# Retention, routed experts and a SoLU layer on one core: router products and masked score products on quarters of the array, two kinds of copies in ScalarE's queue

## The chip, the core and the metric

The kernel runs on one core of a Trainium2 chip. A core has TensorE (matmuls, which read SBUF and write PSUM), VectorE, ScalarE and GpSimd (element-wise work), SyncE (which here issues DMAs), and DMA engines that move data between HBM and SBUF. Each engine takes its own instructions in order; they wait for one another by semaphores. The metric is the time of one execution on the device, in microseconds (us).

## The reference, cut to what matters

Three layers follow one another: retention (attention with a decaying mask and no softmax), a layer of eight experts with one expert per token, and a dense layer with a SoLU and a normalisation. All is 32-bit floating point.

```python
# q, k, v: batch 8, heads 8, sequence 576, head_dim 64
scores = scale * np.matmul(q, k.transpose(0, 1, 3, 2))
Dmat = np.where(rel >= 0, gamma[:, None, None] ** rel[None, :, :], 0.0)
ret = scores * Dmat[None, :, :, :]
attn = np.matmul(ret, v)                      # -> x: 4608 tokens x 512

logits = x @ w_gate                           # 8 experts
expert_idx = np.argmax(logits, axis=1)
gate_w = softmax(logits)[np.arange(N), expert_idx]
out[mask] = gate_w[mask, None] * (np.maximum(x[mask] @ w1[e], 0.0) @ w2[e])   # per expert e

h = x @ w_in                                  # third layer, x is now `out`
e = np.exp(h - h_max); sm = e / (np.sum(e) + 1e-09); solu = h * sm
return ((solu - mu) / np.sqrt(var + 1e-06) * g_ln) @ w_out
```

## The kernel before, in words

**Chunks.** The retention runs over 8 batches of 576 tokens. A batch is cut into four chunks of 128 tokens and a fifth of 64, so there are 40 chunks, n = 0 to 39. The decay lets the mask be split: what a chunk's queries see of earlier chunks goes through a running state (64 x 64 per head), and only the square of a chunk with itself is computed as scores. For each chunk TensorE makes, in this order of the program:

- `scores(n + 1)`, one chunk ahead (line 448): keys by queries for eight heads into two PSUM tiles `ps`; VectorE multiplies each by its part of the decay table, PSUM to SBUF, giving `pp` (line 451, for the 64-token chunk line 453). The two `ps` tiles are all there are, so the next scores wait for that;
- state products (line 481): the state `old` by the scaled queries `qp`, into `po`; not in the first chunk of a batch;
- masked score products (line 493): the values by `pp`, added into the same `po`. Per head these contract over the 128 keys of the chunk and give 64 rows by 128 queries. The decay table is zero where a key comes after the query;
- the state update `upd` (line 472): keys by values into `pu`, which stays in PSUM over a batch; VectorE copies it to SBUF as the next state (line 474). The fifth chunk has none;
- `px` for one token tile (line 528), in `xtile`.

`po` has one buffer. ScalarE copies it to the token tiles `xts` (line 504): a tile holds 128 tokens with features in partitions. In even batches a chunk is just one tile; in odd batches it is the second half of one tile and the first half of the next, in two copies.

**`xtile`** turns a finished tile and finds its expert logits in one go: `xts` is the stationary operand, and the moving operand `wgi` holds, for each block of 128 features, an identity (128 columns) beside the gate weights (8 columns). `px` is tokens by 136 columns per block. A matmul contracts over 128 features and gives 64 tokens, so two of them fill the two column halves of the array. ScalarE copies `px` to `xr` (line 529) in two pieces, each with its own PSUM buffer. A tile is `ready` for this when all its tokens come before the current chunk. `xtile` is called at the end of `chunk(n)`.

**`route`** handles tiles in groups of 8, 8, 8, 4, 4 and 4: it sums the partial logits (line 539), picks the expert, ranks the tokens and builds index lists. It is a generator: `tick(budget)` runs some of its steps on VectorE at the end of each chunk and again after it, each step priced by hand (0.15, or 0.35 for one scaled tile), and a step that needs TensorE waits for the next chunk ("pe"). In `scale` (lines 562 to 584) each tile is multiplied by its gate into `xo`, by ScalarE (line 576) for even tiles and by VectorE (line 578) for odd ones, except in the last group, where ScalarE does all; SyncE then issues the store of a whole group to HBM (line 583). SyncE's queue also holds the chunk loads, `load(n + 7)` after each chunk.

GpSimd scales the keys (line 424) and queries (line 430) of chunk n + 2 in `prep`. From the index lists GpSimd gathers the tokens of each expert (line 368), and the experts (lines 867 to 884) and the third layer follow on TensorE. Some lines: 203, 592 to 596 and 241 are route's small matmuls, 682 and 701 to 702 build `wgi`, 178 and 179 split an expert's weights in two parts.

## Time and profile before

| what | value |
|---|---|
| median of 3 runs | 1051.08 us (1048.8 to 1055.26) |
| the profiled execution's own time | 1045.0 us |
| its span | 1043.2 us |
| TensorE matmuls busy | 1012.7 us, 97% of the span |
| VectorE busy | 648.1 us, 62% |
| ScalarE busy | 449.5 us, 43% |
| GpSimd busy | 231.1 us, 22% |
| mean granted TensorE clock | 0.992 |
| data moved by DMA | 130.79 MB |

The span is from the first to the last instruction of one profiled execution; its own time has some 2 us around that. In the profile PE is TensorE's matmuls, PEld its weight loads (each matmul has one, loaded while an earlier matmul runs), DVE is VectorE, ACT ScalarE, POOL GpSimd, SP SyncE; a q behind the name is the engine's sequencer. L448 is line 448. A matmul of 32-bit data appears as two loads and two matmuls. The retention takes about the first 170 us.

### The profile page before, as it was taken

The page shows a single profiled execution, that of the slowest core. Times are in us where ns is not written, and L with a number is a line of the kernel's source. Part 1 is how long each engine was busy: PE and PEld are TensorE (multiplying, and loading weights), DVE is VectorE, ACT ScalarE, POOL GpSimd, SP SyncE. Part 2 cuts the span into 40 slices and gives each one's busy share as a digit, 9 for nine tenths or more (in the row PEclk, how much of TensorE's full clock was granted, in tenths as well). Part 3 has the DMA queues.
Part 4 walks back from the last instruction along what each step waited for, and adds up shares of the span by engine and source line. Part 5 has one row for each costly group of instructions (what it writes and reads, how often), then busy time and mean ns, then how long its engine had stood idle before and what let it go on. Part 6 is the DMA issues. An engine that isn't in the chain of part 4 may idle for free.

```text
span 1043.2 us, 20687 instructions
## 1 busy us (share of the span) xinstructions
PE 1012.7 (97%) x8110; PEld 918.3 (88%) x8110; DVE 648.1 (62%) x1642; ACT 449.5 (43%) x847; POOL 231.1 (22%) x254
## 2 busy tenths in 40 slices
PE   7999998899999999999999999899999999999997
PEld 6888887899999999999999997788888888888885
DVE  3467777634677787988343427766666666566652
ACT  1344344333344443433333326455545555545542
POOL 3636421210010102010100021332322222322211
PEclk9999999999999999999999999899999999999999
DMA  9977873344363535453423231111112111111001
GB/s 338 367 263 292 328 267 113 109 156 141 116 206 113 177 122 192 140 187 133 140 102 115 93 109 41 47 51 41 51 41 61 49 43 41 51 42 41 31 21 43
DMA packets 51814, 130.79 MB, mean 125 GB/s; under 512 B 6504, under 2 KB 21344, under 8 KB 47872
## 3 DMA queue, kind: packets, MB, share of 16 engines
q1 hardware_dynamic: 45664, 109.98, 30.1%
q0 software_dynamic: 6048, 19.44, 5.6%
q8 instruction: 66, 1.08, 0.4%
q14 instruction: 36, 0.29, 0.1%
HBM read 99.95 MB, written 29.44 MB: 124 GB/s over the span
## 4 chain that ended last, share of the span: by engine, by line
PE 75%; DVE 3%; issue 2%; ACT 1%; DMA 1%; POOLq 0%; POOL 0%; ACTq 0%
PE py L882 21%; PE ph L867 19%; PE pf L1170 16%; PE hx L1072 7%; PE hz L1072 4%; PE hy L1072 4%; PE ptl L1155 3%; PE px L850 2%; DVE wof L1112 1%; DMA x<-xd,src 0%; ACT raw L1115 0%; DVE wof L1085 0%; DMA out_dram<-o__11948,dst 0%; DMA out_dram<-o__12050,dst 0%; ACT raw L1104 0%
## 5 line engine op out<-in xcount | busy, mean ns | idle before, releaser
L882 PE MATMUL py<-hh,wh 128*128 128x344 f32 (+7 forms) x512 | 157.6, 308 | 0.0
L882 PE MATMUL py<-hl,wh 128*128 128x344 f32 (+7 forms) x512 | 154.7, 302 | 0.0
L882 PE MATMUL py<-hh,wl 128*128 128x344 f32 (+7 forms) x512 | 154.5, 302 | 0.0
L368 POOL DMA_INDIRECT x<-xd,src x42 | 43.5, 1036 | 330.6 <-PE px L850 270.9
L869 ACT ACTIVATE hh<-ph 128x344 fp32r<-128x344 f32 (+7 forms) x128 | 54.1, 425 | 116.4 <-PE ph L867 113.6
L179 DVE TENSOR_TENSOR wl<-raw,wh 128x1024 fp32r<-128x1024 f32 x64 | 78.2, 1221 | 31.2 <-ACT wh L178 30.4
L882 PEld LDWEIGHTS py<-hh,wh 128*128 128x128 f32 x512 | 96.4, 188 | 0.1
L882 PEld LDWEIGHTS py<-hh,wl 128*128 128x128 f32 x512 | 96.5, 188 | 0.0
L882 PEld LDWEIGHTS py<-hl,wh 128*128 128x128 f32 x512 | 96.2, 188 | 0.0
L867 PE MATMUL ph<-xh,wh 128*128 128x344 f32 (+7 forms) x512 | 93.7, 305 | 1.3 <-ACT xh L853 1.3
L867 PE MATMUL ph<-xl,wh 128*128 128x344 f32 (+7 forms) x512 | 93.5, 305 | 0.0
L867 PE MATMUL ph<-xh,wl 128*128 128x344 f32 (+7 forms) x512 | 93.4, 305 | 0.0
L870 DVE SCALAR_TENSOR_TENSOR hl<-ph,hh 128x344 fp32r<-128x344 f32 (+7 forms) x128 | 60.1, 471 | 51.0 <-ACT hh L869 50.9
L884 ACT COPY yo<-py 128x344 f32<-128x344 f32 (+7 forms) x64 | 26.4, 413 | 134.8 <-PE py L882 104.8
L1170 PE MATMUL pf<-woh,wh 128*128 128x512 f32 x288 | 76.9, 409 | 4.6 <-ACT wh L1157 4.6
L1170 PE MATMUL pf<-wol,wh 128*128 128x512 f32 x288 | 81.3, 405 | 0.0
L867 PEld LDWEIGHTS ph<-xh,wh 128*128 128x128 f32 x512 | 78.4, 189 | 1.6 <-ACT xh L853 1.5
L1158 DVE TENSOR_TENSOR wl<-ptl,wh 128x512 fp32r<-128x512 f32 x72 | 49.5, 688 | 47.7 <-ACT wh L1157 47.6
L867 PEld LDWEIGHTS ph<-xl,wh 128*128 128x128 f32 x512 | 78.5, 189 | 0.5 <-DVE xl L854 0.5
L867 PEld LDWEIGHTS ph<-xh,wl 128*128 128x128 f32 x512 | 78.4, 189 | 0.0
L1170 PE MATMUL pf<-woh,wl 128*128 128x512 f32 x288 | 71.9, 391 | 0.0
L178 ACT CAST wh<-raw 128x1024 fp32r<-128x1024 f32 x64 | 67.0, 1047 | 0.0
(604 smaller groups left out, 2080.8 us busy)
## 6 DMA issues: line engine op xcount, KB each, us to landing
raw<-in_w_dram SPq DMA_DIRECT2D x64, 512.0 KB
kc<-in_kvc_dram SPq DMA_DIRECT2D x30, 1024.0 KB
yg<-yd SPq DMA_DIRECT2D x72, 128.0 KB
xd<-xo SPq DMA_DIRECT2D x3, 2048.0 KB
f<-in_win_dram SPq DMA_DIRECT2D x16, 256.0 KB
f<-in_wout_dram SPq DMA_DIRECT2D x16, 256.0 KB
kc<-in_kq_dram SPq DMA_DIRECT2D x8, 256.0 KB
xd<-xo SPq DMA_DIRECT2D x2, 1024.0 KB
```

Source lines behind the costliest of these rows:

```text
L178: nc.scalar.copy(wh, raw)
L179: V.tensor_tensor(out=wl, in0=raw, in1=wh.bitcast(F32), op=ALU.subtract)
L368: nc.gpsimd.indirect_dma_start(out=x[:w, i, :], out_offset=None, in_=xd[:rows, :], in_offset=bass.IndirectOffsetOnAxis(ap=src[:w, e * CT + ...
L867: nc.tensor.matmul(ph, w[:, w0 + kb * P:w0 + kb * P + P], xx[:, kb, cc], start=(n == 0), stop=(n == 3 * KD - 1))
L869: nc.scalar.activation(out=hh[:, cc], in_=ph, func=AF.Relu)
L870: V.scalar_tensor_tensor(out=hl[:, cc], in0=ph, scalar=0.0, in1=hh[:, cc].bitcast(F32), op0=ALU.max, op1=ALU.subtract)
L882: nc.tensor.matmul(p, w[:, ff], h[:, cc], start=(n == 0), stop=(n == 3 * NFB - 1))
L884: nc.scalar.copy(yo[:, cc], p)
L1072: nc.tensor.matmul(p, x[:, 2 * a + k], m[:, w, k], start=(first and k == 0 and i == 0), stop=(k == 1 and i == 2), skip_group_check=True)
L1155: nc.tensor.transpose(p[:, kb, :], u[:, f * P:f * P + P], ident)
L1158: V.tensor_tensor(out=ll[:, fs, :], in0=p, in1=lh[:, fs, :].bitcast(F32), op=ALU.subtract)
L1170: nc.tensor.matmul(pfs[t], a[:, f, :], w[f // 2][:, f % 2, :], start=(n == 0), stop=(n == m - 1))
```

## The change

The quarters: a matmul that contracts over 64 rows and gives 64 rows of output uses a quarter of the array, and four of them can stand in it side by side.

- `px`: each block of 128 features is taken as two halves of 64 features; the identity in `wgi` is 64 wide, so a block has 72 columns instead of 136. Sixteen matmuls on quarters take the place of eight on halves. The logits are now the sum of eight parts instead of four, and the features of a tile stand in another order, which the layout of the experts' first weights (made on the host) follows. `px` is one PSUM tile of two banks instead of two of one.
- masked score products: the first 64 queries of a chunk see only its first 64 keys, so their products contract over 64 keys, on quarters (`av_soon`); the last 64 queries keep all 128 keys (`av_late`). The host swaps the two halves of the keys of odd heads, so that the first keys lie in the other partitions.
- `upd` copies the state with ScalarE instead of VectorE.
- `scale` multiplies all tiles with ScalarE.
- `xtile` is called ahead of `chunk(n)`, behind `scores(n + 1)`, instead of at its end.
- `wgi` needs no zeros, and two copies instead of four.

```diff
-        ps_x = ax.enter_context(tc.tile_pool(name="ps_x", bufs=2, space=PSUM))
+        ps_x = ax.enter_context(tc.tile_pool(name="ps_x", bufs=1, space=PSUM))
...
-        wgi = tab.tile([P, KD, P + E], F32, name="wgi")
+        wgi = tab.tile([P, KD, D + E], F32, name="wgi")
...
-                V.tensor_copy(new, pu)
+                nc.scalar.copy(new, pu)
...
+            def av(pr, h2, keys, v, w, cols, first, last):
+                to = h2 ^ pr % 2
+                nc.tensor.matmul(po[HALF[to], pr % 2, pr // 2, cols], kc[keys, VR, v:v + D], w,
+                                 start=(c == 0 and first and pr < 2), stop=(last and pr >= 2), skip_group_check=True)
+
+            def av_soon():
+                for pr in range(NP):
+                    for h2, r in enumerate(HALF):
+                        if c < 4:
+                            av(pr, h2, r, (2 * pr + h2) * D, pp[r, h2, pr, :D], slice(0, D), True, False)
+                        else:
+                            av(pr, h2, r, pr * D, pp[r, 0, pr, :D], slice(0, D), True, True)
+
+            def av_late():
+                for pr in range(NP):
+                    for h2 in range(2):
+                        av(pr, h2, slice(0, P), (2 * pr + h2) * D, pp[:, h2, pr, D:], slice(D, P), False, True)
...
-            for pr in range(NP):
-                for to, r_ in enumerate(HALF):
-                    h2 = to ^ pr % 2
-                    h, r = 2 * pr + h2, HALF[h2]
-                    a, w = (kc[:, VR, h * D:h * D + D], pp[:, h2, pr, :]) if c < 4 else \
-                        (kc[r, VR, pr * D:pr * D + D], pp[r, 0, pr, :cl])
-                    nc.tensor.matmul(po[r_, pr % 2, pr // 2, :cl], a, w, start=(c == 0 and pr < 2), stop=(pr >= 2),
-                                     skip_group_check=True)
+            av_soon()
+            if c < 4:
+                av_late()
             if c < 4 and n != 1:
                 upd()
...
-            if ready:
-                xtile(nx[0])
-                nx[0] += 1
             tick(1.0 if n < NN - 9 else 1.5)
...
-                grp[g] = rt.tile([P, GMAX, KD, P + E], F32, name="xr", bufs=2)
+                grp[g] = rt.tile([P, GMAX, 2 * KD, D + E], F32, name="xr", bufs=2)
...
-            for half in range(2):
-                px = ps_x.tile([P, 2, P + E], F32, name="px")
-                for j in range(2):
-                    kb = 2 * half + j
-                    for r in HALF:
-                        nc.tensor.matmul(px[r, j, :], x[:, kb, r], wgi[:, kb, :], start=True, stop=True)
-                nc.scalar.copy(xr[:, i, 2 * half:2 * half + 2, :], px)
+            px = ps_x.tile([P, 2, DM], F32, name="px")
+            for kb in range(KD):
+                for to, at in ((0, 0), (1, 1), (0, 1), (1, 0)):
+                    nc.tensor.matmul(px[HALF[at], to, kb * (D + E):(kb + 1) * (D + E)], x[HALF[to], kb, HALF[at]], wgi[HALF[to], kb, :],
+                                     start=True, stop=True)
+            for to in range(2):
+                nc.scalar.copy(xr[:, i, to * KD:to * KD + KD, :], px[:, to, :KD * (D + E)].rearrange("p (k n) -> p k n", k=KD))
...
-            V.tensor_reduce(out=l, in_=xr[:, :n, :, P:].rearrange("p t k e -> p t e k"), axis=AX.X, op=ALU.add)
+            V.tensor_reduce(out=l, in_=xr[:, :n, :, D:].rearrange("p t k e -> p t e k"), axis=AX.X, op=ALU.add)
...
-                    x, o_ = xr[:, i, :, :P], xo[:, i]
-                    if fin or i % 2 == 0:
-                        nc.scalar.mul(o_, x, gt[:, i:i + 1])
-                    else:
-                        V.tensor_scalar(out=o_, in0=x, scalar1=gt[:, i:i + 1], scalar2=None, op0=ALU.mult)
+                    x, o_ = xr[:, i, :, :D], xo[:, i]
+                    nc.scalar.mul(o_, x, gt[:, i:i + 1])
...
-        V.memset(wgi[:, :, :P], 0.0)
...
             if n > 1:
                 scores(n + 1)
                 prep(n + 2)
-            chunk(n, ready)
+            if ready:
+                xtile(nx[0])
+                nx[0] += 1
+            chunk(n)
...
-                    V.tensor_copy(wgi[r, 0:KD:2, r], bc(ident[r, r], 1, KD // 2))
-                    V.tensor_copy(wgi[r, 1:KD:2, HALF[1 - h2]], bc(ident[r, r], 1, KD // 2))
+                    V.tensor_copy(wgi[r, :, :D], bc(ident[r, r], 1, KD))
```

## Rows read from the trace of the kernel before

**Rows 1.** Timeline, a steady chunk: start us, us, engine, line, operation [idle before <-releaser].

```profile
36.06 0.97 PEld L448 LDWEIGHTS ps<-kc 64*128 64x128 f32 x16 [0.18 <-issue]
...
37.15 0.43 PEld L481 LDWEIGHTS po<-qp,st 64*64 64x64 f32 x16
...
37.75 0.85 PEld L493 LDWEIGHTS po<-pp,kc 128*64 128x64 f32 x16 [0.17 <-issue]
...
38.57 0.60 PEld L472 LDWEIGHTS pu<-kc 128*64 128x64 f32 x16
...
38.90 0.65 ACT L504 COPY xts<-po 128x256 f32<-128x256 f32 x2 [2.33 <-PE po L493]
39.09 0.90 PEld L528 LDWEIGHTS px<-wgi,xts 128*64 128x64 f32 x16
...
39.36 0.42 DVE L474 COPY st<-pu 128x256 f32<-128x256 f32 x1 [0.82 <-PE pu L472]
...
39.83 0.85 ACT L529 COPY xr<-px 128x272 f32<-128x272 f32 x2 [0.28 <-PE px L528]
```

**Rows 2.** Waits of the weight loads, 5 to 169 us: total us, times, longest.

```profile
PEld ps L448 <- DVE pp L451: 5.6, 10, 1.2
```

**Rows 3.** Timeline, the next chunks: half-chunk scores, then a batch's last chunk.

```profile
40.17 0.54 PEld L448 LDWEIGHTS ps<-kc 64*64 64x64 f32 x16 [0.18 <-issue]
...
40.58 0.47 PEld L481 LDWEIGHTS po<-qp,st 64*64 64x64 f32 x16
...
43.64 0.97 PEld L448 LDWEIGHTS ps<-kc 64*128 64x128 f32 x16 [0.18 <-issue]
...
44.73 0.32 PEld L481 LDWEIGHTS po<-qp,st 64*64 64x64 f32 x16
...
44.96 0.33 PEld L493 LDWEIGHTS po<-pp,kc 64*64 64x64 f32 x16
...
45.35 0.89 PEld L528 LDWEIGHTS px<-wgi,xts 128*64 128x64 f32 x16
...
45.49 0.37 ACT L504 COPY xts<-po 128x256 f32<-128x256 f32 x1 [1.35 <-PE po L493]
...
48.72 0.58 ACT L504 COPY xts<-po 128x512 f32<-128x512 f32 x1 [1.79 <-PE po L493]
```

**Rows 4.** Timeline, the scaling of the first group of eight tiles.

```profile
59.02 1.27 DVE L578 TENSOR_SCALAR xo<-xr,gt 128x512 f32<-128x512 f32 x3
...
59.89 1.95 ACT L576 ACTIVATE xo<-xr,gt 128x512 f32<-128x512 f32 x3
...
63.36 0.72 ACT L576 ACTIVATE xo<-xr,gt 128x512 f32<-128x512 f32 x1
```

**Rows 5.** Windows: stretch, us, busy per engine (instructions), granted clock, DMA share, GB/s.

```profile
145.00:148.00 3.00, 3.00 (x40) 2.88 (x42) 2.69 (x7) 0.23 (x1) 2.66 (x3) 0.74 0.47 174
148.00:150.00 2.00, 2.00 (x26) 1.88 (x24) 1.36 (x5) 2.00 (x5) 0.29 (x1) 0.54 0.00 0
...
187.00:192.00 5.00, 3.53 (x23) 2.96 (x24) 1.65 (x3) 0.99 (x4) 0.00 (x0) 1.00 0.02 8
```

**Rows 6.** Timeline, two long idle pieces of TensorE.

```profile
144.38 0.29 PEld L448 LDWEIGHTS ps<-kc 64*128 64x128 f32 x2 [1.06 <-DVE pp L451]
...
187.94 0.42 PEld L850 LDWEIGHTS px<-cs,x 128*128 128x128 f32 x4 [1.79 <-DMA x<-xd,src]
```

**Rows 7.** Timeline, the start: building wgi, and the scores of chunk 3.

```profile
14.48 0.21 DVE L701 COPY wgi<-cs 64x128 f32<-64x128 f32 x1
...
14.98 0.22 DVE L702 COPY wgi<-cs 64x128 f32<-64x128 f32 x1
...
19.01 1.16 PE L448 MATMUL ps<-kc 64*128 64x128 f32 x16 [0.79 <-DMA kc<-in_kvc_dram]
```

**Rows 8.** Timeline, the end of the retention.

```profile
164.44 0.88 DVE L578 TENSOR_SCALAR xo<-xr,gt 128x512 f32<-128x512 f32 x2
...
167.62 0.20 PEld L203 LDWEIGHTS <-m 128*128 128x128 bf16 x4 [2.69 <-DVE m L195]
```

## The prediction

> **What bounds the kernel now.** The profiled execution took 1045.0 us with a span of 1043.2; the median of the runs shown is 1051.08, so I work with differences and apply them to both. I read the page's parts 1 and 2 first: TensorE is busy 97% of the span, so what counts is TensorE's queue, and of it only the first 170 us, since the change leaves the experts and the last layer as they are. There I read the timeline of a steady chunk, then the waits of the weight loads.

> In a steady chunk TensorE's loads run through without a hole [rows 1]: scores at 36.06, state products (qp by st) at 37.15, masked score products (pp) at 37.75, state update (pu) at 38.57, px at 39.09, the next scores at 40.17 [rows 3]: 1.09 + 0.60 + 0.82 + 0.52 + 1.08 = 4.11 us. So in this stage TensorE sets the pace, and each instruction removed from its queue counts in full, until another engine is late. VectorE is late in places: scores waited 5.6 us in 10 pieces for the masking that frees their PSUM [rows 2].

> **The change part by part.** Each matmul of 32-bit data is two instructions in the trace, so eight matmuls are a set of 16.

> *Quarters.* A set of 16 quarters (64 rows by 64 columns) over 64 columns takes 0.23 us when quarters follow it (44.73 to 44.96) [rows 3]; over 128 columns 0.43, and then 0.17 pass before halves (all rows by 64 columns) may load [rows 1]. Halves over 128 columns take 0.82, over 64 columns 0.52, over 136 columns 0.90 and 0.18 before the scores [rows 1].
> - px: before 0.90 (16 halves over 136). After 32 quarters over 72: 2 x 0.23 x 72/64 = 0.52. Its two copies stay two, of 288 columns for 272.
> - masked score products: before 0.82. After 16 quarters over 64, 0.23, the 0.17 of the change of shape, and 16 halves over 64: between 0.41 (half of 0.82) and 0.52 (the pu row); I take 0.46.
> - pu is now last, so its 0.52 is followed by the 0.18 before scores.

> The chunk becomes 1.09 (scores) + 0.52 + 0.43 + 0.23 + 0.17 + 0.46 + 0.70 = 3.60, a gain of 0.51. The first chunk of a batch has no state products: 3.51 before, 3.17 after, 0.34 gained in the three that have a px; the four without px lose 0.07. The last chunk of a batch (quarters already) went 43.64, 44.73, 44.96, 45.35 and 1.08 more, 2.79 [rows 3]; after 1.09 + 0.52 + 0.23 + 0.23 + 0.18 = 2.25, 0.54 gained. Of the 24 chunks between I leave out chunk 1, whose order is its own. Sum: 23 x 0.51 + 3 x 0.34 - 4 x 0.07 + 8 x 0.54 + 0.4 (the last px) = 17.1 us gained. Bounds: 13 with all sets at their upper row, 19 with the lower.

> The row shows 16 quarters in 0.23 us, 14 ns from start to start [rows 3]. [...]

> *px moved ahead of the chunk, state copy and po copy in one queue.* This adds a wait. Before, px(n) came a whole chunk after the copy of po that it reads. Now it follows scores(n+1) directly, and that copy stands in ScalarE's queue behind the state copy, which waits for pu. From the start U of pu: the state copy can start at U + 0.79 (39.36 - 38.57) [rows 1] and takes 0.37 (ScalarE's copy of 128x256 at 45.49) [rows 3]; then po, 0.58 in one piece (48.72) [rows 3] or two in 0.65, of which px needs the first [rows 1]. x is ready at U + 1.80 in an even batch, U + 1.55 in an odd one, 0.06 for the signal included. px is due at U + 0.70 + 1.09 = U + 1.79: just covered. But before the fourth chunk of a batch the scores are those of the half chunk and last 0.41 (40.17 to 40.58) [rows 3]: px due at U + 1.11, a wait of 0.69 in four batches and 0.44 in four, 4.5 us; with 0.05 for 12 close cases, 5.1. Bounds: 0 if something else holds TensorE there, 9 if ScalarE's copies take VectorE's 0.42. Behind the waiting px stand state products, masked products and the next pu, nobody can pass.

> Here the rows show VectorE's state copy done beside px with ScalarE free [rows 1]. [...]

> *Scaling.* 16 multiplications leave VectorE and go to ScalarE. They come in lumps: three on VectorE and three on ScalarE in one chunk (1.95 us for ScalarE's three, 0.65 each), then one and one [rows 4]. Now six stand in a row: 3.9 us after the po copy (U + 1.74), to U + 5.64. Behind them stand the px copies of the next chunk (0.85) [rows 1], its state copy (0.37), its po copy (0.58): U + 7.44. The px after that is due at U + 1.79 + 3.60 = U + 5.39 and waits 2.1 us. Three groups of eight: 6.3; 0.3 more where the last chunk's po is late; the fourth group (four tiles, where VectorE is late anyway) 0.8. Sum 7.4; bounds 2 and 10. The xd DMA, which SP must issue before the next chunk load, comes some 1.3 us later; loads run seven chunks ahead by the code (load(n + 7)), so I take nothing for it; without that cover it would be 1.3 a lump, 4 in all.

> [...]

> *VectorE* loses 32 state copies and 16 multiplications, and gains a reduction over twice the columns in six groups. Its waits of 5.6 us do not vanish: the chunk gets shorter by 0.51 and VectorE's work in it by 0.42, so the late masks stay as late; only those right behind a scaling lump go, since the new wait lies there. I take 1.5 gained and 0.5 lost to the reductions; bounds 5.6 gained, 2 lost.

> *The ends.* At the start wgi, built on VectorE at 14.48 to 15.2, is now needed by the px ahead of chunk 1, and TensorE waits for it; but scores(3) wait 0.79 us for their load at 19.01 anyway [rows 7], and the products that the new wait delays have that room and the shorter px's. I take nothing; bounds 0 and 1.7 (a fall of the clock). At the end TensorE waits 2.69 us for one-hots that stand behind two multiplications of 0.88 [rows 8]: 0.9 gained.

> Sum: -17.1 + 5.1 + 7.4 + 2.6 - 1.5 + 0.5 - 0.9 = -3.9. Profiled execution 1041.1, median 1047.2. A measurement of this kernel can tell about 1% (10.5 us) from no change, so this counts as the same.

> **The rivals.**
> - *ScalarE keeps up.* The copies come early enough and the lumps break up over chunks: -17.1 - 1.5 - 0.9 = -19.5, about 1032. For it: ScalarE idles over 2 us ahead of most po copies [rows 1]. Against: that idle lies ahead of the po copy, while the new wait comes behind it. A half-way case, with only the lumps gone, gives -11 to -14.
> - *The narrow quarters run no faster than pu does.* pu takes 0.52 for 16, 32 ns each [rows 1]; at that pace px takes 1.04 and the early products 0.52: 36 x 0.52 + 32 x 0.29 = 28 us back, +24, 1075. At half of it, 14 back, +10. It decides from 18 ns per instruction on. Against it: the 0.23 of the last chunk [rows 3]. [...]
> - *The clock falls after every wait of px.* Three lumps and eight short waits at 1.7 us each [rows 5]: 18.7 for 2.6, so +12, about 1063. Slower than before from five falls on. For it: 1.06 us was enough once [rows 6]; against: 1.79 was not.

> **How the numbers follow.** My forecast 0.70, ScalarE keeps up (or half-way) 0.20, narrow quarters 0.05, the clock 0.05. The likeliest is 1047 us. The forecast's own range is 1040 to 1055; the range reaches towards the first rival, to 1033, and, for the clock and the quarters, up to 1060. Faster by over 1% (under 1040.6): 0.20 of the first rival and 0.04 of the forecast, 0.24; slower by over 1%: both slow rivals, less their milder half, and a little of the forecast, 0.09; within 1%: 0.67.

> **What would show it.** Steady chunks 3.6 us from scores to scores; px loads of 32 in about 0.52 and early products in 0.23. In the waits, a new line of px behind ScalarE's xts copy, some 12 to 14 us in all, with one piece near 2 us behind each scaling lump and pieces near 0.7 and 0.4 in the fourth chunk of each batch. The end of the first stage some 4 us earlier than now, and all that follows moved with it. It is wrong if that line is under 5 us, if the quarters take over 0.3 per 16, or if the clock shows more than four stretches at the lower level before 170 us.

## The result, and the profile after

The changed kernel took 1064.01 us (median of 4 runs, 1062.79 to 1066.22) beside 1050.88 us for the kernel before on the same chip: a ratio of 1.0122 with a 95% interval of 1.0085 to 1.0159. It is slower, and outside the range of the prediction. The profiled execution has a span of 1061.0 us, 17.8 longer than before (1043.2). That is more than the 13.1 us between the medians, because the profiled execution before, at 1045.0 us, was faster than every other of its kernel; what follows accounts for these two executions. All of the 17.8 arises before 178 us: the scores of the last chunk start 18.2 us later, as TensorE's timelines of before and after show, and what follows them takes as long as it did (883.6 us before, 883.1 after).

```profile
159.67 0.55 PEld L448 LDWEIGHTS ps<-kc 64*64 64x64 f32 x16 [0.86 <-PE pm L203]
```

```profile
177.92 0.55 PEld L458 LDWEIGHTS ps<-kc 64*64 64x64 f32 x16 [0.87 <-PE pm L213]
```

First the steady chunk, in TensorE's timeline of the changed kernel (L458 scores, L547 px, L491 state products, L496 both parts of the masked products, L482 state update):

```profile
36.80 0.97 PEld L458 LDWEIGHTS ps<-kc 64*128 64x128 f32 x16
37.89 0.58 PEld L547 LDWEIGHTS px<-wgi,xts 64*64 64x64 f32 x32
38.38 0.43 PEld L491 LDWEIGHTS po<-qp,st 64*64 64x64 f32 x16
38.77 0.99 PEld L496 LDWEIGHTS po<-pp,kc 64*64 64x64 f32 x32
39.68 0.55 PEld L482 LDWEIGHTS pu<-kc 128*64 128x64 f32 x16
...
40.30 0.30 PEld L458 LDWEIGHTS ps<-kc 64*128 64x128 f32 x4
```

From scores to scores it is 3.50 us, where [rows 1] and [rows 3] have 4.11 and 3.60 was predicted. px went from 1.08 with its change of shape to 0.49, and both parts of the masked products take 0.91 (0.86 predicted). Between the scores of chunk 3 and those of the last chunk I took out of the timeline every idle piece of TensorE's weight loads of over 0.24 us: of 140.7 us before 132.7 are left, of 157.8 after 124.6. Some 8.5 of these 124.6 are lost to the clock (below). So by this estimate the quarters gave 16.6 us, close to the 17.1 that were predicted for all chunks.

The time went into holes: idle pieces in the middle of work. Four of them, in TensorE's timeline:

```profile
33.73 0.14 PEld L491 LDWEIGHTS po<-qp,st 64*64 64x64 f32 x4 [2.26 <-issue]
...
43.76 0.30 PEld L491 LDWEIGHTS po<-qp,st 64*64 64x64 f32 x9 [1.67 <-issue]
...
82.70 0.14 PEld L491 LDWEIGHTS po<-qp,st 64*64 64x64 f32 x3 [3.55 <-issue]
...
88.76 0.82 PEld L496 LDWEIGHTS po<-pp,kc 64*64 64x64 f32 x23 [2.37 <-issue]
```

They lie in the middle of a set, and "issue" says that the engine waited for nothing that the profile shows: no operand, no buffer. The windows between them, in the changed kernel (columns: stretch, length, busy per engine with instructions, granted clock, DMA share, GB/s):

```profile
27.59:33.73 6.13, 4.02 (x127) 3.62 (x126) 1.29 (x2) 2.26 (x6) 5.52 (x5) 1.00 1.02 398
33.73:43.76 10.03, 8.61 (x253) 7.66 (x253) 3.87 (x6) 3.62 (x11) 6.33 (x7) 1.00 0.84 302
82.69:88.75 6.06, 3.76 (x126) 3.34 (x127) 2.33 (x4) 1.62 (x5) 4.26 (x4) 1.00 0.98 401
```

The first two numbers in brackets are TensorE's matmuls and weight loads: 253 of each in the middle window, 506 together, and half as many in the two others. The windows leave out the semaphore instructions that stand between them in TensorE's queue; with these it is 512 from 33.73 to 43.76, 255 and 257 in the two others. Counted like this from the start, all 12 such holes lie at instruction 194 of a block of 256 (one place either way), 21.7 us together; before there was 0.26 us at one such place. The third part of the page names what comes in such portions, here of the changed kernel and of the one before:

```profile
q8 instruction: 74, 1.21, 0.5%
```

```profile
q8 instruction: 66, 1.08, 0.4%
```

That is 1.21 MB in 74 packets of 16 KB each. TensorE's 18572 instructions (2 x 9198 loads and matmuls and 176 others) make 72.5 blocks of 256; before, 16365 made 63.9, with 66 packets. So I take a packet to be one block of TensorE's, by estimate from these counts; no row of the profile names the receiver of q8, the counts and the times below are the ground for it. The DMA view of the changed kernel shows when one travelled, in the middle of the run. TensorE passed a boundary between two blocks at 82.70; up to 86.30 the engines moved only data (first view), then the packet comes (second view), and the next block starts at 88.76, where a hole of 2.37 us ends:

```profile
DMA packets 211, 1.49 MB, mean 414 GB/s; under 512 B 29, under 2 KB 29, under 8 KB 29
...
q1 hardware_dynamic: 211, 1.49, 98.9%
```

```profile
q1 hardware_dynamic: 337, 0.92, 94.7%
q8 instruction: 1, 0.02, 2.6%
```

By the packets' records the next piece started 0.6 to 0.9 us after TensorE passed a boundary where the DMA engines moved nothing (at 70.06, 106.55, 165.04 and 179.33; a fifth time, at 155.32, it took 3.2 us, with TensorE idle for most of them just behind the boundary). It started 2.4 to 5.3 us after the boundary ahead of each of the 12 holes, where the engines were at 91% or more; a hole ended 2.2 to 2.6 us after the packet started. So ahead of these holes a piece of 256 instructions took 4.8 to 7.9 us to come, and on idle engines, as an estimate from the same figures, about 3. Before, a chunk of 160 TensorE instructions lasted 4.11 us, a piece 4.11 x 256/160 = 6.6. Now it has 224 in 3.50, a piece 4.0: less than the 4.8 to 7.9 that the supply took ahead of the holes.

The waits of the weight loads, 5 to 188 us of the changed kernel (total us, times, longest); beside them stands the line of [rows 2]:

```profile
PEld po L491 <- issue: 10.6, 6, 3.6
PEld px L547 <- issue: 9.4, 6, 2.2
PEld ps L458 <- DVE pp L461: 5.1, 4, 3.0
PEld px L547 <- ACT xts L528: 5.0, 9, 1.6
...
PEld po L496 <- issue: 4.2, 4, 2.4
```

The "issue" lines hold the holes and 2.5 us more: the first px's wait for `wgi` (1.87 us at 14.59) and short pieces. ScalarE's lumps are there as foreseen, six scalings in a row where [rows 4] had three, with their followers (ScalarE's timeline):

```profile
64.09 3.79 ACT L596 ACTIVATE xo<-xr,gt 128x512 f32<-128x512 f32 x6
67.77 0.68 ACT L550 COPY xr<-px 128x288 f32<-128x288 f32 x2
68.34 0.38 ACT L484 COPY st<-pu 128x256 f32<-128x256 f32 x1
68.61 0.60 ACT L528 COPY xts<-po 128x512 f32<-128x512 f32 x1
```

The clock, windows of the kernel before and then of the changed one:

```profile
100.00:170.00 70.00, 64.13 (x1227) 55.96 (x1224) 53.52 (x147) 28.93 (x70) 21.74 (x21) 0.98 0.75 270
170.00:215.00 45.00, 40.41 (x251) 38.62 (x250) 27.94 (x86) 18.00 (x33) 9.15 (x9) 0.96 0.33 106
```

```profile
100.00:170.00 70.00, 54.53 (x1502) 48.89 (x1498) 42.92 (x93) 35.10 (x85) 25.44 (x23) 0.90 0.69 249
170.00:215.00 45.00, 38.41 (x483) 35.20 (x484) 26.05 (x94) 19.14 (x42) 6.37 (x6) 0.85 0.33 109
```

The granted clock stood at 1.00 or at 0.50 (0.50 from 118.7 to 122.0, for one). A mean of 0.90 over 70 us is 14 us at 0.50. Up to the last chunk's scores it is 23.9 us, where before it was 3.4: some 10 us of work lost, if TensorE would have been busy in it, 8.5 of them behind the scores of chunk 3.

Between the scores of chunk 3 and those of the last chunk, TensorE's idle pieces grew from 8.0 us to 33.1, by 25.1: 21.4 are the holes at the 256th instruction, 4.4 px's waits for ScalarE, 1.2 one piece at 156.99 that no run explains, and the waits for masks shrank by 1.8 (5.1 for 6.9, the half chunks' masks included). The rest fell from 132.7 to 124.6, by 8.1: -16.6 for the quarters and 8.5 for the clock. The scores of chunk 3 start 1.2 later, with px's wait for `wgi` ahead of them. 25.1 - 8.1 + 1.2 = 18.2, as measured.

### The profile page after: what moved, and what is told of

Same layout as the page of the kernel before. It is cut to its first block, busy times and chain, and to the rows that moved or that the text cites. A ratio compares the mean times of both kernels' runs of the same rounds, so it can differ in the third digit from the quotient of the medians.

```text
span 1061.0 us, 22896 instructions
## 1 busy us (share of the span) xinstructions
PE 1005.5 (95%) x9198; PEld 914.7 (86%) x9198; DVE 635.3 (60%) x1591; ACT 464.7 (44%) x895; POOL 233.8 (22%) x254
## 3 DMA queue, kind: packets, MB, share of 16 engines
q8 instruction: 74, 1.21, 0.5%
## 4 chain that ended last, share of the span: by engine, by line
PE 74%; DVE 3%; issue 2%; ACT 1%; DMA 1%; POOLq 0%; POOL 0%; ACTq 0%
PE py L901 20%; PE ph L886 19%; PE pf L1189 16%; PE hx L1091 6%; PE hz L1091 4%; PE hy L1091 4%; PE ptl L1174 3%; PE px L869 1%; DVE wof L1131 1%; DMA x<-xd,src 0%; ACT raw L1134 0%; DVE wof L1104 0%; DMA out_dram<-o__12453,dst 0%; DMA out_dram<-o__12555,dst 0%; ACT raw L1123 0%
## 5 line engine op out<-in xcount | busy, mean ns | idle before, releaser
L378 POOL DMA_INDIRECT x<-xd,src x42 | 44.0, 1048 | 340.3 <-PE px L869 274.6
L461 DVE TENSOR_TENSOR pp<-ps,dt_t 128x512 f32<-128x512 f32 x64 | 41.1, 684 | 47.8 <-PE ps L458 47.8
```

What stands on the lines that cost most here:

```text
L378: nc.gpsimd.indirect_dma_start(out=x[:w, i, :], out_offset=None, in_=xd[:rows, :], in_offset=bass.IndirectOffsetOnAxis(ap=src[:w, e * CT + ...
L461: V.tensor_tensor(out=pp[:, h2], in0=ps[h2], in1=dtc[:, h2], op=ALU.mult)
```

## The experiments

In what follows A is: TensorE's instructions come in pieces of 256, and behind other transfers a piece comes too late. B is: ScalarE's queue and the clock alone. "Holes" are those at the 256th instruction, summed from the timeline of one profiled execution each. A "chunk" is the time of a steady chunk from scores to scores without holes.

**One part at a time.** The changed kernel with the masked products whole again, so that only px is in quarters (192 instructions per chunk):

```
-            av_soon()
-            if c < 4:
-                av_late()
+            for pr in range(NP):
+                for to, r_ in enumerate(HALF):
...
```

> The changed kernel with the masked score products whole again (eight halves over 128 columns), all else as changed: 192 TensorE instructions a steady chunk instead of 224 (before: 160), and a steady chunk of 3.6 us instead of 3.50 where nothing waits. Theory A (TensorE runs out of instructions, which it gets in pieces of 256 by a DMA that stands behind the chunk loads; a piece lasted about 6 us before, 4.0 after): a piece lasts 4.8 us, so the holes at every 256th instruction shrink from 21.6 us to 8 to 12, and the time falls to 1050 to 1056. Theory B (ScalarE's queue and the clock made the loss): the holes between 256 instructions do not depend on the number of instructions, the time rises by about 4 us, to 1066 to 1069.

Measured 1054.67 us, 1.0065 of before (1.004 to 1.009); 14.6 us of holes, where A expected 8 to 12, and chunk 3.68. And the kernel before with the early and late masked products alone (192 too, ScalarE and VectorE as before):

```
+            av_soon()
+            if c < 4:
+                av_late()
-            for pr in range(NP):
...
```

> The kernel before with nothing but the early and late masked score products (av_soon, av_late): 192 instructions a steady chunk, px still on halves, state copies and odd scalings on VectorE, px at the end of the chunk. Steady chunk about 4.0 us, a piece of 256 lasts 5.3 us. Theory A: a few holes at the 256th instruction, 2 to 6 us in all, and no gain left: ratio to before 0.997 to 1.003. Theory B: no holes, 3 to 4 us gained, ratio 0.996 or less.

Measured 1055.97 us, 1.0065 (1.0035 to 1.0096); 11.2 us of holes, more than either expected. This kernel has no work moved to ScalarE, and it is slower than before although its steady chunk is 3.9 instead of 4.11: its weight loads wait for "issue" where nothing of ScalarE's is in the way, as here in its timeline, between the early and the late half of the masked products:

```profile
77.48 0.43 PEld L489 LDWEIGHTS po<-qp,st 64*64 64x64 f32 x16
79.58 0.36 PEld L493 LDWEIGHTS po<-pp,kc 64*64 64x64 f32 x16 [1.67 <-issue]
```

**ScalarE's share.** The changed kernel with state copies and odd tiles' scaling back on VectorE:

```
-                nc.scalar.copy(new, pu)
+                V.tensor_copy(new, pu)
...
+                    if fin or i % 2 == 0:
+                        nc.scalar.mul(o_, x, gt[:, i:i + 1])
+                    else:
+                        V.tensor_scalar(out=o_, in0=x, scalar1=gt[:, i:i + 1], scalar2=None, op0=ALU.mult)
```

> The changed kernel with the state copies and the odd tiles' scaling back on VectorE; TensorE's instructions as changed. Theory A: the holes at every 256th instruction stay, 17 to 23 us, and the time stays above the kernel before: 1054 to 1062 (the waits of px on ScalarE's copy, 5 us, and the wait behind the weight cast, 3 us, go). Theory B: the loss goes, 1040 or less.

Measured 1063.76 us, 1.0155 (1.0107 to 1.0204): no better than the change, and just above the 1054 to 1062 that A expected; 21.4 us of holes. Its waits, 5 to 188 us:

```profile
PEld po L491 <- issue: 11.0, 8, 2.0
PEld ps L458 <- DVE pp L461: 8.8, 11, 1.6
PEld px L547 <- issue: 6.9, 6, 2.9
PEld po L496 <- issue: 6.0, 6, 2.3
```

px's 5.0 us for ScalarE are gone from the list; 3.7 of it came back as masks that are late. B's part on ScalarE falls with this run: moving its work back takes away 1.3 us of waits. The clock's part does not: up to the last scores 20.5 us are at the granted 0.50 here, 23.9 in the change.

**Fewer bytes.** The changed kernel that from chunk 12 on loads only the KR quarter of each chunk, and nothing of the fifth chunks (what it then computes of the rest is from old data, so only the retention is compared):

```
...
+            elif n >= 12:
+                if c < 4:
+                    nc.sync.dma_start(kc[:, KR], kvc[b, c, :, KR * DM:(KR + 1) * DM])
...
```

> The changed kernel, but from chunk 12 on only a quarter of each chunk's operands is loaded (the key rows that are scaled in place), the rest is what the buffer held; the output is not the reference's, and after the first stage the tokens fall to other experts, so only the first stage is compared. TensorE's instructions are the same in number and order. Theory A (the instruction pieces come late because they stand behind the chunk loads): from 50 us on the holes at the 256th instruction fall from 15.5 us to under 5, and the scores of the last chunk start at 155 to 164 us instead of 177.9. If the pieces come late whatever else the DMA does, the holes stay at 12 or more. Theory B: the last scores start after 170.

One execution: 1052.66 us (the kernel before, on the same chip, 1047.62). The scores of the last chunk start at 167.8, where A expected 155 to 164 and B later than 170. From 50 us to 155 the DMA share is 0.41 where the change has 0.80, and the holes in it fall from 15.5 to 7.3 us. Of the four that are left (2.2, 2.5, 0.3, 2.3 us) the three large ones lie some 10 us behind the issue of a group's 2 MB store of xd. The direction is A's; the size lies between, and the stores, which were left, are the likely reason.

**More instructions.** The kernel before with 16 one-column products per tile that nobody reads:

```
+                for _ in range(4):
+                    for r in HALF:
+                        nc.tensor.matmul(px_[r, 500:501], ones[:, :D], ones[:, :1], start=True, stop=True, skip_group_check=True)
```

> The kernel before with 16 extra TensorE products of one column per tile (32 more instructions per chunk, 192 instead of 160), into a column of px's bank that nobody reads; nothing else changes, and the output stays the same. Theory A (TensorE's instructions arrive in pieces of 256, and behind chunk loads and xd stores a piece comes too late once 256 instructions last under some 6 us): the kernel before, which showed only two such holes of .2 us, gets holes at every 256th TensorE instruction, 4 to 12 us together; with the extra products' own time (32 instructions at 14 to 25 ns are .45 to .8 us per chunk, 40 chunks: 18 to 32 us at most, less what fits under waits) 1065 to 1090. Theory B (the loss comes from ScalarE's queue and the clock alone): no such holes, only the extra products' own time.

Measured 1061.75 us, 1.0119 (1.0084 to 1.0154), below the 1065 to 1090 expected, and 7.95 us of holes in seven places, as A has it. One of them, in the middle of the state update, and the chunk after it, in its timeline:

```profile
33.43 0.48 PEld L472 LDWEIGHTS pu<-kc 128*64 128x64 f32 x10
34.94 0.31 PEld L472 LDWEIGHTS pu<-kc 128*64 128x64 f32 x6 [1.03 <-issue]
...
35.31 0.97 PEld L448 LDWEIGHTS ps<-kc 64*128 64x128 f32 x16
...
39.73 0.97 PEld L448 LDWEIGHTS ps<-kc 64*128 64x128 f32 x16 [0.18 <-issue]
```

Nothing of the change is in this kernel but the number of instructions. This is the run that shows where the holes come from. They are not its whole loss: the extra products also take time of their own, 4.42 us a chunk for 4.11, which is 10 ns for each of the 32 instructions; the expectation took 14 to 25, and the quarters of the traces show 14 (0.23 us for 16, [rows 3]) and 24 (the state products of the steady chunk above, 0.39 for 16). From the scores of chunk 3 to those of the last chunk it is 13.8 us longer than before: 9.2 for that time, 7.7 for holes, and 3.0 less in other waits.

**Fewer instructions.** The masked products alone as above, and px as one product per block over the whole array (176 per chunk):

```
-                    for r in HALF:
-                        nc.tensor.matmul(px[r, j, :], x[:, kb, r], wgi[:, kb, :], start=True, stop=True)
+                    nc.tensor.matmul(px[:, j, :], x[:, kb, :], wgi[:, kb, :], start=True, stop=True)
```

> The early and late masked products of the change, without its other parts, in the kernel before, and px as one product per block over the whole array in place of two halves: 176 TensorE instructions per chunk, where the same without the whole px has 192 and lost 11.2 us in holes at the 256th instruction. Theory A: a piece of 256 then lasts about .09 longer, and the holes fall to 5 us or less, the time to 1046 to 1053 (.996 to 1.002 of before). Theory B: as the run with 192, 1.0065 of before.

Measured 1057.93 us, 1.0082 (1.005 to 1.0115): a miss. The holes fell from 11.2 to 6.6 us, but px over the whole array takes 1.12 with its change of shape, which takes the chunk back to 4.12. What was gained in supply was lost in the array. In the profiled execution what follows the last scores is 4.2 us longer than before; no run explains that part.

**What the piece waits for.** The changed kernel, and the kernel before as control, with each 1 MB load as four and each group's store as one DMA per tile:

```
...
-                nc.sync.dma_start(kc, kvc[b, c].rearrange("p (a f) -> p a f", a=4))
+                for a in (KT, Q, KR, VR):
+                    nc.sync.dma_start(kc[:, a], kvc[b, c, :, a * DM:(a + 1) * DM])
...
```

> The changed kernel with each chunk load as four DMAs of 256 KB instead of one of 1 MB, and each group's xd store as one DMA of 256 KB per tile. Nothing else changes. Theory A1 (the piece of instructions waits for the DMA that is in progress on the engine that fetches it): holes at the 256th instruction fall from 21.7 to under 8 us and the time to 1035 to 1050. Theory A2 (it waits for all the transfers that are queued ahead): holes about 20 us as in the changed kernel, time 1058 to 1068. Theory B (the loads have no part in it): 1062 to 1066.

> The control: the kernel before with the same small DMAs. It has next to no holes at the 256th instruction, so by theory A1 and A2 the time stays within .3% of the kernel before; a gain of as much as the changed kernel's would say that small DMAs help by another way than the supply of instructions.

Measured 1070.33 us, 1.0202 (1.0167 to 1.0236), with 28.4 us of holes, and for the control 1.0002 (0.9967 to 1.0038). A1 falls: small DMAs did not let the piece through sooner. The time and the holes are above what A2 expected, too. The delay from a boundary to the packet was hardly shorter (median 2.9 us where the DMA engines were over half busy, 3.1 in the change), and 26 pieces met such engines where it had been 23.

Then the store alone: tile by tile, issued by ScalarE behind its scaling, in four kernels (the change; the change with each load as four DMAs besides; px in quarters only; the kernel before):

```
...
-                    if fin:
-                        nc.sync.dma_start(xd[(f + i) * P:(f + i + 1) * P, :], o_.rearrange("p k d -> p (k d)"))
+                    (nc.sync if fin else nc.scalar).dma_start(xd[(f + i) * P:(f + i + 1) * P, :], o_.rearrange("p k d -> p (k d)"))
...
```

> The changed kernel with xd stored tile by tile (256 KB), each store issued by ScalarE right behind the product that scales the tile, in place of one 2 MB store per group in SyncE's queue, where chunk loads queue up behind it and then go out three at a time. Theory A2 (a piece of TensorE's instructions waits for all that is queued ahead of it): the holes that lie some 10 us behind a group's store (82.7, 88.8, 117.7, 124.0, 149.8, 155.3 in the changed kernel, 11.7 us together) mostly go, those behind single chunk loads stay: 8 to 13 us of holes in place of 21.7, time 1052 to 1058. A1 (it waits for one DMA in progress): a smaller fall, 15 to 19 us of holes. If the supply of instructions does not hang on the backlog: 20 us or more, 1061 to 1067.

> The run before this one with each chunk load as four DMAs of 256 KB besides, so that the quarters whose readers are done early go out early. A2: backlogs are shorter still, 5 to 11 us of holes, 1047 to 1057. If small packets are what made the run with small DMAs worse (2 KB rows take .087 us each where 8 KB rows take .31), it comes out above the run before this one, by 2 to 6 us.

> px in quarters with the masked products whole (192 TensorE instructions per chunk; 14.6 us of holes and 1.0065 of before when run alone) and the stores by ScalarE, tile by tile. A2: 4 to 8 us of holes, 1046 to 1051 (.995 to 1.000 of before): the one of these kernels that might beat the kernel before. If the backlog has no part in it: 13 us or more of holes, 1.005 or more.

> The control: the kernel before with the same stores by ScalarE. It has next to no holes, so A2 gives it nothing by the supply of instructions: .997 to 1.004 of before. A gain of over .5% would say that the stores cost the kernel before something else, such as loads that come late.

Measured 1.0233, 1.0344, 1.0202 and 1.0108 of before, all slower than expected; the second is 11.7 us slower than the first, where 2 to 6 were given for the cost of small packets. The holes did fall, to 13.5, 16.4 and 4.1 us in the first three, but ScalarE pays for the issue. Its timeline in the control, and the wait of px in the first of them:

```profile
100.15 0.72 ACT L576 ACTIVATE xo<-xr,gt 128x512 f32<-128x512 f32 x1
100.91 0.81 ACTq L579 DMA_DIRECT2D xd<-xo  x2
101.76 0.72 ACT L576 ACTIVATE xo<-xr,gt 128x512 f32<-128x512 f32 x1 [0.89 <-DVE xo L578]
```

```profile
PEld px L547 <- ACT xts L528: 14.2, 8, 5.6
```

Two stores cost 0.81 us of its queue. In the first of these kernels a lump of six scalings with their stores lasts 6.7 us (63.70 to 70.43) where it was 3.8, and px waits 14.2 us where it waited 5.0. In the control ScalarE also waits for VectorE's tiles before it can issue their stores, and three times TensorE's state products wait 1.9 to 2.2 us and start right behind ScalarE's late copy of `po`. The list calls these waits "issue" as well, but none of them lies at a 256th instruction.

Last, the same stores from SyncE's queue, each right behind its scaling (the line of the diff above with nc.sync throughout): the change, px alone, px alone with copies and scaling on VectorE, and the kernel before.

> The changed kernel with xd stored tile by tile from SyncE's queue, each store placed right behind its scaling, so that ScalarE issues nothing. A2 (the piece of instructions waits for the backlog of the DMA engines): 10 to 15 us of holes at the 256th instruction in place of 21.7, as with the stores by ScalarE, and without ScalarE's cost of issue 1052 to 1058. If the shorter backlog there came only from TensorE being held up by ScalarE, the holes stay at 19 us or more and the time at 1061 to 1067.

> px in quarters, the masked products whole (192 instructions per chunk), stores tile by tile from SyncE's queue. A2: 4 to 9 us of holes in place of 14.6, time 1046 to 1052 (.995 to 1.001 of before). Without an effect of the backlog 1.005 or more.

> The same with the state copies and the odd tiles' scaling back on VectorE, so that ScalarE's copies for px are not queued behind them (px waited 5.0 us for ScalarE in the changed kernel). Holes 4 to 9 us, time 1043 to 1050: better than the kernel before, if both causes are what they seem. If VectorE's masks are then what comes late, 1048 to 1056.

> The control: the kernel before with the same stores. It has no holes to lose, so .997 to 1.003 of before; what it gains beyond that is not the supply of instructions.

| kernel | holes, us | median, us | ratio to before |
|---|---|---|---|
| the change, stores per tile | 17.3 | 1062.75 | 1.0112 (1.0056 to 1.0168) |
| px alone, stores per tile | 8.2 | 1055.21 | 1.0048 (1.0023 to 1.0074) |
| the same, copies and scaling on VectorE | 9.9 | 1051.26 | 1.0022 (1.0001 to 1.0044) |
| before, stores per tile | 0.0 | 1048.58 | 0.9979 (0.996 to 0.9998) |

Holes shrink here without ScalarE's issues, from 21.7 to 17.3 and from 14.6 to 8.2, so part of the fall goes with stores that are spread out; the rest of the fall in the runs before, to 13.5 and 4.1, came with a TensorE that ScalarE held up. That the backlog is what shrank is argued, not shown. The 10 to 15 us expected for the first were too few, and the times of the second and third lie above the 1046 to 1052 and 1043 to 1050 that were expected. No version with quarters beats the kernel before; the kernel before with stores per tile is the fastest, by 0.2%, at the edge of what was measured.

## Why the prediction was wrong

- *The quarters* were right: 17.1 us predicted, 16.6 found by the estimate above; the steady chunk 3.50 for 3.60. The rival of narrow quarters did not come: 32 loads in 0.49 us are 15 ns each.
- *The step that failed* is in the first part: "in this stage TensorE sets the pace, and each instruction removed from its queue counts in full, until another engine is late". The change removes streaming time and no instructions; it adds 64 to the 160 of a chunk, and the supply of instructions was a limit beside the engines. It was in no term of the sum and in no rival. Before, q8 stood on the page with 66 packets, 0.4% of the DMA engines' time, and TensorE lost only 0.26 us to them. The term left out is 21.4 us, more than the whole gain.
- *px behind ScalarE* was mis-sized. 5.1 for single waits and 7.4 for the lumps were predicted, 12.5 in all; the list shows 5.0 in nine pieces. The largest piece behind a lump is 1.63 us, for 2.1; the signal, taken at 0.06, was 0.05 from the end of ScalarE's copy to px's loads. TensorE was late itself in the holes, which gave ScalarE time; in the run with fewer bytes, whose holes from 50 us on were 8.2 us shorter, px waited 6.4 us for ScalarE from there on, where it waits 4.3 in the change.
- *The clock* was mis-sized: the sum takes 2.6, and about 10 was found. No run shows the 2.6: up to the last scores the kernel before had one stretch of 3.4 us at a granted 0.50 [rows 5], 1.7 us of work, and the change has 23.9 us. The rival had it by the waits of px alone; of the stretches at 0.50, that at 118.7 follows a hole, those at 16.3 and 142.6 follow px's waits for wgi and ScalarE, and the long ones at 156.2 and 169.9 lie among holes and late masks. The sign of failure that the prediction named, more than four such stretches before 170 us, came true: five begin before it, three of 3.4 us and two of 6.8. Idleness alone did not bring them: the longest hole, 3.55 us at 82.70, was followed by none.
- *VectorE*: 1.0 gained was predicted, the waits for masks shrank by 1.8. *The start*: px waited 1.87 us for wgi at 14.59, just above the upper bound named (1.7); nothing was taken for it. *The end*: 0.9 gained was predicted. The wait for one-hots fell only from 2.69 to 2.33 us. Before it, four scalings at 164.49 on ScalarE delay a cast of the expert's weights, VectorE's next product waits for that cast, the masks stand behind it, and TensorE waits 2.96 us for them at 169.91.
- *State copies and scaling on ScalarE alone*: the run with them back on VectorE took 5.0 us of px's waits away and gave 3.7 back in masks; the time got no better (1063.76 us). With px alone in quarters and stores per tile it was worth 4 us (1055.21 to 1051.26, with intervals that overlap).

What stays open is on what exactly the delay of a piece hangs. Fewer bytes and stores that are spread out left smaller holes (7.3 us for 15.5, 17.3 for 21.7), smaller DMAs did not (28.4); whether it is the number of packets ahead, the order in which the queues are served or memory, no run here tells. How much of the clock's loss would go with the holes is open too.

## What to carry to other kernels

Count instructions, not only busy time: where a change cuts wide products into narrow ones, work out how long 256 of TensorE's instructions last (here 6.6 us before, 4.0 after) and hold it against the time that a piece took to come, here about 3 us on idle DMA engines (an estimate) and 4.8 to 7.9 ahead of the holes, behind loads and stores. Holes "<-issue" in the middle of a set of like instructions, at multiples of 256 instructions from one another with the semaphore instructions counted, were that supply here; "issue" alone was also a wait that the profile does not name, as the three of 1.9 to 2.2 us behind ScalarE's copy of `po`. With loads running nearly all the time (a DMA share of 0.80 from 50 us to 155), narrower products that add instructions lost what they saved: 16.6 us gained, 21.4 us of holes.
